# Seven block products for w2 in both halves of a fused attention and MLP kernel, two steps at a time

## The chip, the core and the metric

The kernel runs on one core of a Trainium2 chip. The time is that of the device in microseconds (us). Five engines work side by side, each with its own queue in program order: PE (matmuls; its weight loads are the row PEld), DVE and ACT (elementwise work, both read PSUM), POOL (elementwise work on SBUF) and SP, which here issues nearly all DMAs. Semaphores alone hold an engine back.

## The reference

With S = 2048 rows, D = 576 columns and F = 4608 hidden columns, float32:

```
x = A_x
g = sigmoid((x * gate_w).sum(-1))
a = linear_attention(x, wqkv, wo)        # 32 heads of 18 columns
y = layernorm(x)
h = gelu(y @ w1 + b1)
b = h @ w2 + b2
out = g * a + (1 - g) * b
```

## The kernel before

**Precision.** An operand is split in a high part (rounded to the matmul's format, by ACT) and a low part (the rest, subtracted by DVE). A product is the sum of high x high, high x low and low x high (`TERMS`).

**Stages.** A sweep over the 16 row tiles makes keys, queries and sums; `at(n, ...)` places jobs in it, among them four pairs of row tiles of normalised x (`load_pair`, `normal_pair`, `sum_pair`, `split_pair`, `store_pair`). Each pair is split and stored to `yd` in DRAM. Then comes attention, one row tile per turn of a loop; `extra[i]` places jobs after turn i. Then the MLP: 36 steps k. The first 18 go over w1's 18 chunks of 256 hidden columns for rows 0 to 1023 (first half), the other 18 over the same chunks for rows 1024 to 2047 (second half).

**The product with w1** is done in blocks of two by two with seven products in place of eight (Strassen's scheme): for each, `product` issues seven matmuls of 512 columns with an operand of `wa` or `wb` (w1) and one of `Y`. Four PSUM banks go round: X takes products 1, 6, 7 and 4, with copies by ACT between; Yb takes 2, Z takes 5 and 3. The operands of w1 are loaded (`load_w1`), summed on POOL (`sum_w1`), split (`split_w1`) and stored to `w1d` in the first half, and read back in the second.

**The product with w2** runs one step behind. In the first half `down` adds it for each of eight row tiles: 12 matmuls of 288 columns into a pair of banks, which DVE adds to `acc[s]`, attention's result, scaled by 1 - g. The steps 18 to 33 of the second half use seven products here too: POOL sums blocks of w2 (`sum_w2`) and of h (`sum_h`), ACT and DVE split them, `unit` issues six matmuls, and DVE (in the first step ACT for some) adds each result to `sums` in SBUF. The steps 34 and 35 are done plainly at the end, and `add_combined` puts the sums together. Attention's rows of the second half wait in DRAM (`late_acc`).

**Order.** Every engine gets its instructions in the order of the code. In the first half the other four pairs of row tiles are made between the down products (`after`).

Of the kernel before, what the change touches and what calls it, by code (L numbers as in the profile page):

```python
# [17 lines left out]
P = 128  # L18
# [16 lines left out]
GATES = ((0, 8), (8, 16))  # L35
EPS_PHI = 1e-6
# [76 lines left out]
def tile_gated_mix(ctx: ExitStack, tc: tile.TileContext, x, xm, xe, wm, we, wvm, wve, wo, um, ue, w2, b1, b2, gw, out):  # L113
# [39 lines left out]
    for _ in range(WARM):  # L153
# [11 lines left out]
    sums = {n: accs[:, i * TPB * HALF:(i + 1) * TPB * HALF].rearrange("p (s n) -> p s n", n=HALF)  # L165
            for i, n in enumerate(DOWN_ORDER)}
# [11 lines left out]
    late_acc = dram.tile([TPS, P, D], F32, name="late_acc")  # L178
# [205 lines left out]
    rows = spare[:, :4 * P].rearrange("p (a n) -> p a n", a=2)  # L384
    yr = spare[:, 4 * P:25 * P].rearrange("p (m s n) -> p m s n", m=7, s=3)

    def load_pair(sup, j):
        q = sup * TPS + 2 * j
        for a, m in enumerate((B11, B12)):
            i = ORDER[q + a]  # L390
            own = yr[:, m:m + 2]
# [161 lines left out]
    for j, (scaled, loaded, *parts) in enumerate(((9, 13, 18, 19, 20, 21), (14, 20, 25, 27, 28, 29),  # L553
                                                  (22, 28, 33, 34, 35, 36), (27, 35, 41, 42, 44, 45))):
        prepare_scale(j, scaled)
        at(loaded, load_pair, 0, j)
        for a in range(2):
            for k in range(2):
                at(loaded + 3 + a, normal_pair, 0, j, a, k)
        for m in range(4):  # L560
            at(parts[m // 2], sum_pair, 0, j, m)
        for part, n in enumerate(parts):
            at(n, split_pair, 0, j, part, lambda part=part: y_stages[part])
            at(n, split_tails, 0, j, part)
# [174 lines left out]
    def attend_out(i):  # L739
        act.activation(halves(acc[i]), abank[i][:, :, :HALF], AF.Identity, scale=g[:, PLACE[i]:PLACE[i] + 1])  # L740
        if i >= TPS:
            sp.dma_start(late_acc[i - TPS], acc[i])


    hs, c2s, w2raw = {}, {}, {}

    def wr(k):
        at_ = fresh[:, :24 * P] if k > 1 else spare[:, :24 * P]
# [38 lines left out]
    def w2_rows(k):  # L787
        c = k % NCHUNK
        return w2[c * CF * P:(c + 1) * CF * P].rearrange("(f p) d -> p f d", p=P)

    def load_w2(k, to):
        w2raw[k] = to.rearrange("p (f n) -> p f n", f=CF)
        sp.dma_start(w2raw[k], w2_rows(k))

    def split_w2(k, to, parts=(0, 1)):
        c2 = c2s[k] = to.rearrange("p (a f n) -> p a f n", a=2, f=CF)
        if 0 in parts:
            act.activation(c2[:, 0], w2raw[k], AF.Copy)
# [15 lines left out]
    def kept(p):  # L814

        t = up.tile([P, SB], F32, name="u")
        act.activation(t, p, AF.Copy)
        return t

    def plus(t, p):  # L820
        dve.tensor_tensor(out=t, in0=p, in1=t, op=OP.add)
        return t

    def gelu(k, f, t, src, whole, h=None, split=True):

        bias = b1s[:, k % NCHUNK * CF + f:k % NCHUNK * CF + f + 1]
        if split:
            h = hs[k, f, t] = take_h((k, f, t)) if h is None else h
            act.activation(h[:, 0], src, AF.Gelu_apprx_tanh, bias=bias)
        act.activation(whole, src, AF.Gelu_apprx_tanh, bias=bias)  # L830
        return lambda: dve.tensor_sub(h[:, 1], whole, raw(h[:, 0]))

    TERMS = ((0, 0), (0, 1), (1, 0))
    terms = [(f, a, w) for f in range(CF) for a, w in TERMS]

    def add(i, to, term):
        dve.scalar_tensor_tensor(to, term, omg[:, PLACE[i]:PLACE[i] + 1], to, op0=OP.mult, op1=OP.add)

    def down_terms(p, s, k, half, only=range(len(terms)), opens=True, closes=True):
        c0 = s % TPB * P  # L840
        for n in only:
            f, a, w = terms[n]
            pe.matmul(p, hs[k, f, s // TPB][:, a, c0:c0 + P], c2s[k][:, w, f, half_cols(half)],
                      start=opens and n == 0, stop=closes and n == len(terms) - 1)

    def down(k, s):

        if k >= 0:
            p = two_of(ff_pairs)[:, :, :HALF]
            for n in range(len(terms)):  # L850
                for half in range(2):
                    down_terms(p[:, half], s, k, half, (n,))
            if s % TPB == TPB - 1:
                give_back_h((k, 0, s // TPB), (k, 1, s // TPB))
            add(s, halves(acc[s]), p)
            if k == 1 + s:
                add(s, acc[s], b2b)
            if k == HALF_TIME - 1:
                sp.dma_start(out[s * P:(s + 1) * P, :], acc[s])
        for job in later.get((k + 1, s), ()):  # L860
            job()

# [44 lines left out]

    fresh = ctx.enter_context(tc.tile_pool(name="fresh", bufs=1)).tile([P, 33 * P], F32, name="fresh")
    region = ctx.enter_context(tc.tile_pool(name="region", bufs=1)).tile([P, 56 * P], F32R, name="region")
    y_stage = [region[:, n * 10 * P:(n + 1) * 10 * P].rearrange("p (m s n) -> p m s n", m=2, s=5) for n in range(2)]  # L910
    w2_whole = fresh[:, 24 * P:33 * P]
    c2_places = [region[:, (20 + 18 * n) * P:(38 + 18 * n) * P] for n in range(2)]
    w2_sums = fresh[:, :7 * HALF].rearrange("p (m n) -> p m n", n=HALF)
    s_places = [region[:, 14 * HALF + n * 2 * SB:][:, :2 * SB].rearrange("p (a n) -> p a n", a=2)
                for n in range(3)]
    load_w2(0, w2_whole)

    later = {}

    def after(k, s, f, *args):  # L920
        later.setdefault((k + s // 8, s % 8), []).append(lambda: f(*args))

    for j in range(TPB):
        k, s = divmod(15 + 28 * j, TPS)
        after(k, s, load_pair, 1, j)
        for n in range(4):
            after(k, s + 6 + n, normal_pair, 1, j, n // 2, n % 2)
            after(k, s + 10 + n, sum_pair, 1, j, n)
        for part in range(4):
            after(k, s + 14 + 3 * part, split_pair, 1, j, part, lambda part=part: y_stage[part % 2])  # L930
            after(k, s + 15 + 3 * part, split_tails, 1, j, part)
# [13 lines left out]
    for k in range(HALF_TIME):  # L945
        X, Yb, Z = bank(), bank(), bank()
        if k:
            split_w1(k, False)
# [275 lines left out]
```

## Time and profile before

| | us |
|---|---|
| median of 3 runs (1125.62 to 1129.38) | 1129.38 |
| the profiled execution | 1128.42 |
| its span, first to last instruction | 1126.7 |

Line numbers in the profile mean little here, since a helper on one line records every operation (L109): groups go by tiles. A group's row gives the operation, out<-in with shapes, its count, busy us, mean ns of one, and idle time ahead of it with what ended it. A row of the timeline gives the start, the time to the last one's end, engine, operation and count. A row by stages gives the stage, its length, then busy us and count for PE, PEld, DVE, ACT and POOL, the granted clock, the DMA engines' share and GB/s. `spare`, `acc` of the first half and `sums` are parts of the tile `accs`; raw w1 and w2 lie in `fresh`.

### The profile page before, as it was taken

Reading aid. Unit: us, or ns where it says so; the run is one execution under the profiler, and the core shown is the slowest. Engines: PE = TensorE matmul, PEld = TensorE weight load, DVE = VectorE, ACT = ScalarE, POOL = GpSimd, SP = SyncE. Lnnn points to the kernel's source line nnn. Section 1 sums busy time; section 2 is a strip of 40 time slices with the busy share of each in tenths; the row PEclk is TensorE's granted clock in tenths of the full one; section 3 lists DMA queues with packets and bytes.
Section 4 is the critical chain, followed back from the end, with each engine's and each line's share of the span. In section 5 each row is a group of like instructions: output and inputs, shape, how many; then the busy total and the mean of one; then the engine's idle time right before and its main releaser. Section 6 shows DMA issues by size and latency. Waiting matters only on the chain.

```text
span 1126.7 us, 18078 instructions
## 1 busy us (share of the span) xinstructions
PE 1114.1 (99%) x6867; PEld 1022.0 (91%) x6867; DVE 861.9 (76%) x1297; ACT 545.5 (48%) x933; POOL 308.6 (27%) x255
## 2 busy tenths in 40 slices
PE   8999999999999999999999999999999999999998
PEld 8999988999899999999999999988999899989988
DVE  4567776885678878778768765678898889888985
ACT  6566655443545444535544543455444544454441
POOL 1111112342111123112122111234453445344520
PEclk9999999999999999999999999999999999999999
DMA  6466765834455764555655549744444444444452
GB/s 175 148 115 176 175 164 99 298 120 143 168 168 179 234 209 160 205 172 190 235 193 174 190 166 390 286 134 124 122 136 137 120 123 137 134 121 124 137 175 84
DMA packets 106252, 189.84 MB, mean 168 GB/s; under 512 B 12351, under 2 KB 61247, under 8 KB 101942
## 3 DMA queue, kind: packets, MB, share of 16 engines
q1 hardware_dynamic: 105602, 188.10, 53.3%
q8 instruction: 54, 0.88, 0.3%
q10 hardware_dynamic: 564, 0.59, 0.2%
q14 instruction: 32, 0.26, 0.1%
HBM read 121.93 MB, written 66.73 MB: 167 GB/s over the span
## 4 chain that ended last, share of the span: by engine, by line
PE 90%; DMA 3%; DVE 3%; ACT 2%; issue 1%; SPq 1%; ACTq 0%
PE ps L109 90%; DMA t<-in_xe 2%; DMA accs<-in_xe 1%; DVE accs L109 1%; SPq L109 1%; DVE u L109 0%; DMA s<-in_wm 0%; DVE region L109 0%; ACT y L109 0%; ACT h L109 0%; ACT u L109 0%; DVE ys L109 0%; DVE wp L109 0%; ACT e L109 0%; DVE den L109 0%
## 5 line engine op out<-in xcount | busy, mean ns | idle before, releaser
L109 PEld LDWEIGHTS ps<-region,h 128*128 128x128 f32 x2568 | 368.5, 188 | 22.7 <-DVE accs L109 1.0
L109 PE MATMUL ps<-region,h 128*128 128x288 f32 x2568 | 383.1, 295 | 0.5 <-DVE region L109 0.2
L109 PE MATMUL ps<-y,wa 128*128 128x512 f32 x1008 | 265.0, 392 | 0.0
L109 POOL TENSOR_TENSOR fresh<-fresh 128x384 f32<-128x384 f32 (+1 forms) x128 | 136.9, 1075 | 439.0 <-DMA fresh<-in_ue 277.0
L109 PE MATMUL ps<-y,wb 128*128 128x512 f32 x756 | 200.9, 394 | 1.0 <-ACT u L109 1.0
L109 PEld LDWEIGHTS ps<-y,wa 128*128 128x128 f32 x1008 | 177.8, 188 | 26.2
L109 DVE TENSOR_TENSOR accs<-ps,accs 128x576 f32<-128x576 f32 x210 | 158.2, 753 | 32.3 <-PE ps L109 22.6
L109 ACT ACTIVATE h<-u,b1s 128x512 fp32r<-128x512 f32 x90 | 65.3, 725 | 214.7 <-DVE u L109 214.7
L109 PEld LDWEIGHTS ps<-y,wb 128*128 128x128 f32 x756 | 132.9, 188 | 23.0 <-ACT u L109 1.7
L109 DVE SCALAR_TENSOR_TENSOR accs<-ps,omg,accs 128x576 f32<-128x576 f32 (+1 forms) x146 | 118.2, 810 | 44.3 <-PE ps L109 43.3
L109 ACT ACTIVATE u<-ps 128x512 f32<-128x512 f32 x108 | 63.8, 591 | 150.2 <-PE ps L109 150.0
L109 POOL TENSOR_TENSOR u<-u 128x512 f32<-128x512 f32 x64 | 100.3, 1567 | 126.1 <-ACT u L109 122.3
L109 PE MATMUL ps<-y 128*128 128x288 f32 (+1 forms) x896 | 127.5, 300 | 2.8 <-ACT y L109 1.6
L109 PEld LDWEIGHTS ps<-y 128*128 128x128 f32 x896 | 124.4, 192 | 5.3 <-ACT y L109 2.3
L109 DVE TENSOR_TENSOR h<-u,h 128x512 fp32r<-128x512 f32 x142 | 104.7, 737 | 27.3 <-ACT u L109 27.1
L109 ACT ACTIVATE u<-u,b1s 128x512 f32<-128x512 f32 x108 | 78.2, 724 | 53.9 <-DVE u L109 50.9
L109 DVE TENSOR_TENSOR u<-ps,u 128x512 f32<-128x512 f32 x108 | 74.2, 687 | 36.5 <-ACT u L109 23.4
L109 PEld LDWEIGHTS ps<-region 128*128 128x128 f32 x600 | 90.3, 188 | 8.9 <-ACT accs L109 0.5
L109 DVE TENSOR_TENSOR region<-fresh,region 128x576 fp32r<-128x576 f32 (+1 forms) x83 | 82.0, 987 | 20.7 <-ACT region L109 19.2
L109 PE MATMUL ps<-region 128*128 128x288 f32 x600 | 96.2, 295 | 0.1
L109 PE MATMUL ps<-wp,qt 128*128 128x288 f32 x448 | 63.3, 298 | 0.3 <-DVE qt L109 0.3
L109 PEld LDWEIGHTS ps<-wp,qt 128*128 128x128 f32 x448 | 59.9, 188 | 0.5 <-DVE qt L109 0.5
(131 smaller groups left out, 1039.6 us busy)
## 6 DMA issues: line engine op xcount, KB each, us to landing
w1d<-wa SPq DMA_DIRECT2D x18, 1280.0 KB
wa<-w1d SPq DMA_DIRECT2D x72, 320.0 KB
y<-yd SPq DMA_DIRECT2D x14, 1280.0 KB
w1d<-wb SPq DMA_DIRECT2D x18, 960.0 KB
wb<-w1d SPq DMA_DIRECT2D x54, 320.0 KB
fresh<-in_w SPq DMA_DIRECT2D x20, 576.0 KB
fresh<-in_w SPq DMA_DIRECT2D x32, 288.0 KB
fresh<-in_um SPq DMA_DIRECT2D x64, 128.0 KB
```

Source lines behind the costliest of these rows:

```text
L109: return lambda *args, **kwargs: self.tc.keep_in_program_order(op(*args, **kwargs))
```

## The change

- `unit` now serves both halves. Two steps make a window of 14 slots, one product with w1 each; a window's units are those of the window before. A unit adds both steps (j = 0, 1) in PSUM, 12 matmuls of 288 columns, before DVE adds it to its place in `accs`. The last window alone is done plainly.
- h is kept whole for two steps in `ups`. Gelu runs once, not twice; ACT's high part and DVE's low part are made for both steps in one instruction, 1024 wide, in two operand places used in turn; those of w2 likewise (576 wide). POOL sums h in the first half too.
- In each slot the six matmuls of j = 0 stand inside the product with w1, but after product 7 both pieces stand behind it.
- Attention's rows of both halves go to `late_acc` and come back at the end of each half, in `w1_raw`.
- All eight pairs of row tiles are made ahead: five in the sweep, two in attention (POOL normalises them), the last in the first window, which has no units. The load of w1 for step 1 moves from attention to that window.

The core of the diff:

```diff
+PAIRS_IN_SWEEP = 5
...
-        sp.dma_start(late_acc[i - TPS], acc[i])
+        sp.dma_start(late_acc[i], acc[i])
...
+    def unit(p, x, j):
+        m, q = divmod(x, 2)
+        if j == 0:
+            unit_bank[p, x] = two_of(ff_pairs)[:, :, :HALF]
+        to, place = unit_bank[p, x], (7 * p + m) % 2
+        for i, (a, b) in enumerate(TERMS):
+            for n in range(2):
+                c0 = (2 * q + n) * P
+                pe.matmul(to[:, n], h_ops[:, place, j, a, c0:c0 + P], w2_ops[:, place, b, j],
+                          start=j == 0 and i == 0, stop=j == 1 and i == len(TERMS) - 1)
...
+    for k in range(HALF_TIME):
+        w, odd = divmod(k, 2)
+        if k:
+            do(w, (1, 7)[odd], split_w1, k, False)
+            do(w, (3, 9)[odd], store_w1, k, False)
+        if k + 1 < HALF_TIME:
+            do(w, (1 if k else 0, 7)[odd], load_w1, k + 1)
+            do(w, (3, 9)[odd], sum_w1, k + 1)
+            do(w, (5, 11)[odd], split_w1, k + 1, True)
+            do(w, (6, 13)[odd], store_w1, k + 1, True)
...
+        for m in range(7):
+            do_first(w, 2 * m - 2, prepare_hi, p, m)
+            do(w, 2 * m - 2, prepare_h_lo, p, m)
+            do(w, 2 * m - 2, prepare_w2_lo, p, m)
+        for x, m in ((0, S3), (3, S2), (6, S1), (7, S4)):
+            do(w, x, sum_h, p, m)
...
+    for w in range(WINDOWS):
+        for x in range(14):
+            k, i = 2 * w + x // 7, x % 7
...
+            product(k, n, into[n], n in (1, 2, 5), range(0, 4))
+            run_jobs(w, x, 0)
+            if w and n != 7:
+                unit(w - 1, x, 0)
+            product(k, n, into[n], n in (1, 2, 5), range(4, 7))
+            finish_up(k, n, into)
+            if w:
+                for j in range(n != 7, 2):
+                    unit(w - 1, x, j)
+                unit_out(w - 1, x)
+            run_jobs(w, x, 1)
```

Three places show how instructions move. On SP, around the loads of raw w1 for the second step (`in_um`, `in_ue`), before:

```order
L109 DMA w1d_112<-wa 128x2560
L109 DMA late_acc<-acc_87 128x576
L109 DMA late_acc<-acc_88 128x576
L109 DMA accs<-in_um 128x2x128
L109 DMA accs<-in_ue 128x1x128
```

and in the changed kernel:

```order
L111 DMA late_acc<-acc_94 128x576
L111 DMA w_raw<-in_um 128x2x128
L111 DMA w_raw<-in_ue 128x1x128
...
L111 DMA accs<-moments_111 128x512
L111 DMA w1d_112<-wa 128x2560
L111 DMA w2r<-in_w 128x2x288 x4
L111 DMA w1d_112<-wb 128x1920
```

The loads stood after the store of attention's tenth row tile (`acc_88`). Now they stand after that of the last (`acc_94`) and ahead of the row factors (`moments`), the stores of w1 for the first step and w2. The first of them waits for the stores of the last rows, which lie in the memory that `w_raw` takes.

On POOL, from the end of attention (`qz` are products for a row tile's weights) into the MLP, before:

```order
L109 TENSOR_TENSOR qz<-acc_93,pks 128x576
L109 TENSOR_TENSOR qz<-acc_94,pks 128x576
L109 TENSOR_TENSOR accs<-accs 128x384 x4
L109 TENSOR_TENSOR fresh<-fresh 128x384 x64
L109 TENSOR_TENSOR fresh<-fresh 128x288 x4
```

and in the changed kernel:

```order
L111 TENSOR_TENSOR accs<-accs 128x768
L111 TENSOR_TENSOR qz<-acc_94,pks 128x576
L111 TENSOR_TENSOR accs<-accs 128x384 x8
L111 TENSOR_TENSOR accs<-accs 128x768
L111 TENSOR_TENSOR w_raw<-w_raw 128x384 x4
L111 TENSOR_TENSOR accs<-accs 128x768 x3
L111 TENSOR_TENSOR accs<-accs 128x384 x4
L111 TENSOR_TENSOR w_raw<-w_raw 128x384 x4
L111 TENSOR_TENSOR w2r<-w2r 128x576 x4
L111 TENSOR_TENSOR u<-u 128x512 x2
```

Where sums of w1 alone filled the first half, normalising the last pair (768 wide), its sums (384) and those of w2 (576) and h (512) now stand in one queue with them; one 768 stands ahead of the sums for step 1.

On DVE, a piece of the first half, before (one step in part):

```order
L109 TENSOR_TENSOR h<-u,h 128x512
L109 TENSOR_TENSOR wa<-fresh,wa 128x4x256
L109 TENSOR_TENSOR wa<-fresh,wa 64x4x128
L109 TENSOR_TENSOR u<-ps,u 128x512
L109 SCALAR_TENSOR_TENSOR accs<-ps,omg,accs 128x576
L109 TENSOR_TENSOR accs<-accs 128x768
```

and in the changed kernel:

```order
L111 TENSOR_TENSOR h<-u,h 128x2x512
L111 TENSOR_TENSOR w_ops<-w2r,w_ops 128x576
L111 TENSOR_TENSOR accs<-ps,accs 128x576
L111 TENSOR_TENSOR wa<-w_raw,wa 128x4x256
L111 TENSOR_TENSOR wa<-w_raw,wa 64x4x128
L111 TENSOR_TENSOR u<-ps,u 128x512
L111 TENSOR_TENSOR accs<-ps,accs 128x576
L111 TENSOR_TENSOR h<-u,h 128x2x512
L111 TENSOR_TENSOR w_ops<-w2r,w_ops 128x576
```

The low parts of h are twice as wide, those of w2 stand behind each, and evictions of units (`accs<-ps,accs`) take the place of `down`'s additions.

More of the change, by code (lines that the diff above doesn't have):

```diff
@@ L812, in product @@
                 load_split_w1(k + 1, a)
[L814 to L861, printed above, removed]
+    upper = accs[:, spare.shape[1]:]
     weigh(3)
@@ L909, in tile_gated_mix @@
[L909 to L931, printed above, removed]
-            after(k, s + 16 + 3 * part, store_pair, 1, j, part)
@@ new lines, in add, with load_late, add_combined @@
+    def add(i, to, term):
+        dve.scalar_tensor_tensor(to, term, omg[:, PLACE[i]:PLACE[i] + 1], to, op0=OP.mult, op1=OP.add)
+    late_tiles = [w1_raw[:, n * D:(n + 1) * D] for n in range(5)] + [pks, b2b]
+    def load_late(i, place):
+        sp.dma_start(late_tiles[place], late_acc[i])
+    def add_combined(p, i, place):
+        s = i % TPS
+        m0, m1 = (SLOTS[p // HALF_PAIRS][n] for n in ((2, 3), (4, 7))[s // TPB])
+        c = accs.rearrange("p (m s n) -> p m s n", m=7, n=HALF)[:, :, s % TPB]
+        add(i, halves(late_tiles[place]), c[:, m0:m1 + 1:m1 - m0])
@@ L958, in tile_gated_mix @@
-        low11 = gelu(k, 0, 0, u1, u1)
-        down(k - 1, 1)
-        low11()
-        product(k, 6, X, False)
-        u2 = kept(X)
-        if k:
-            split_w2(k, c2_places[k % 2])
-        if k < HALF_TIME - 1 and k:
-            load_w2(k + 1, w2_whole)
-            sum_w1(k + 1)
-        elif k:
-            load_w2_blocks(k + 1)
-            for n in range(4):
-                sum_w2(n)
-        down(k - 1, 2)
-        product(k, 5, Z)
-        if not k:
-            split_w1(1, True)
-            store_w1(1, True)
@@ L1061, in add_combined @@
-    def add_combined(s):
-        c = accs.rearrange("p (m s n) -> p m s n", m=7, n=HALF)[:, :, s % TPB]
-        m0, m1 = (DOWN_ORDER.index(n) for n in ((2, 3), (4, 5))[s // TPB])
-        add(TPS + s, halves(late_tiles[s]), c[:, m0:m1 + 1:m1 - m0])
-    def add_sums(engine, to, x):
-        engine.tensor_tensor(out=sums[to], in0=sums[to], in1=sums[x], op=OP.add)
-    late_tiles = [fresh[:, n * D:(n + 1) * D] for n in (0, 1, 4, 5, 6)] + [pks, b2b, accs[:, 0:D]]
-    UP_ORDER = (1, 2, 6, 5, 7, 4, 3)
@@ new lines, in tile_gated_mix, with down_terms @@
+    run_jobs(WINDOWS, 0, 0)
+    run_jobs(WINDOWS, 0, 1)
+    p = WINDOWS - 1
+    tail_pairs = cycle((next(ff_pairs), next(ff_pairs), 0, 2))
+    def down_terms(to, s, half):
+        terms = [(f, j, a, b) for f in range(CF) for j in range(2) for a, b in TERMS]
+        c0 = s % TPB * P
+        for n, (f, j, a, b) in enumerate(terms):
+            w = w2_tail(((B11, B12), (B21, B22))[f][half])
+            yield lambda n=n, f=f, j=j, a=a, b=b, w=w: pe.matmul(
+                to, h_tail((f, s // TPB))[:, j, a, c0:c0 + P], w[:, b, j], start=n == 0, stop=n == len(terms) - 1)
@@ L1164, in tile_gated_mix @@
     for s in range(TPS):
         i, to = TPS + s, late_tiles[s]
-        if s >= len(held):
-            add_combined(s)
-        steps = (LAST,) if s < len(held) else (PLAIN, LAST)
+        pair = two_of(tail_pairs)[:, :, :HALF]
+        add_combined(p, i, s)
         if s < TPS - 1:
-            p = held[s] if s < len(held) else two_of(ff_pairs)[:, :, :HALF]
-            for k in steps:
-                for n in range(len(terms)):
-                    for half in range(2):
-                        down_terms(p[:, half], s, k, half, (n,), k == PLAIN, k == LAST)
-            add(i, halves(to), p)
-            if s == 0:
-                lows[3]()
-            sp.dma_start(out[i * P:(i + 1) * P, :], to)
+            for both in zip(*(down_terms(pair[:, half], s, half) for half in range(2))):
+                for mm in both:
+                    mm()
+            add(i, halves(to), pair)
+            store_out(i, s)
@@ L1179, in tile_gated_mix @@
         else:
             for half in range(2):
-                p = bank()[:, :HALF]
-                for k in steps:
-                    down_terms(p, s, k, half, opens=k == PLAIN, closes=k == LAST)
-                add(i, to[:, half_cols(half)], p)
+                for mm in down_terms(pair[:, half], s, half):
+                    mm()
+                add(i, to[:, half_cols(half)], pair[:, half])
                 sp.dma_start(out[i * P:(i + 1) * P, half_cols(half)], to[:, half_cols(half)])
```

459 lines of the change are left out of this document (228 added, 231 removed).

## The prediction

> **What bounds the kernel now.** The page's busy row and its chain that ended last come first, then the waits of PE.
>
> ```profile
> PE 1114.1 (99%) x6867; PEld 1022.0 (91%) x6867; DVE 861.9 (76%) x1297; ACT 545.5 (48%) x933; POOL 308.6 (27%) x255
> PE 90%; DMA 3%; DVE 3%; ACT 2%; issue 1%; SPq 1%; ACTq 0%
> ```
>
> PE is busy for 99% of the span and holds 90% of the chain. A busy PE alone proves little, since its ends are modelled, so the waits decide:
>
> ```profile
> PE ps L109 <- DMA accs<-in_gw: 2.2, 1, 2.2
> PE ps L109 <- ACT y L109: 1.6, 2, 1.5
> ```
>
> The longest wait of PE in the whole run is 2.2 us, at the start. Five stages matter here: most of the sweep over the row tiles, attention, first half, the last step of that half, and second half. In each row: length, then busy us of PE, PEld, DVE, ACT and POOL, clock, DMA share and GB/s.
>
> ```profile
> 62.00:165.00 103.00, 101.93 (x681) 97.53 (x680) 74.87 (x160) 63.53 (x147) 17.00 (x14) 1.00 0.67 164
> 206.20:278.20 72.00, 71.68 (x552) 71.45 (x553) 57.36 (x96) 31.98 (x71) 24.87 (x20) 1.00 0.54 208
> 338.80:674.10 335.30, 335.30 (x2032) 306.24 (x2031) 262.75 (x352) 161.02 (x213) 70.29 (x56) 1.00 0.57 191
> 674.10:698.10 24.00, 24.00 (x148) 21.93 (x147) 14.57 (x20) 10.33 (x15) 0.84 (x2) 1.00 1.00 384
> 813.20:1061.50 248.30, 248.30 (x1465) 223.87 (x1465) 219.55 (x310) 117.39 (x198) 108.74 (x88) 1.00 0.44 129
> ```
>
> PE is full in each of them. DVE is next: 262.75 of 335.3 us in the first half (78%), 219.55 of 248.3 in the second (88%). So matmuls taken away are worth their whole pace, as long as no other engine makes PE wait instead.
>
> **Term 1, the matmuls.** Before, first-half products with w2 take 18 steps of 8 x 2 x 6 = 96 matmuls, second-half units 16 steps of 84, and the two last steps 96 each: 3264. Afterwards 17 windows of two steps take 7 x 2 x 2 x 6 = 168 and the last window 192: 3048. So 216 of 288 columns go. Their pace, from PE's timeline:
>
> ```profile
> 701.28 1.77 PE L109 MATMUL ps<-y,wa 128*128 128x512 f32 x7
> 702.89 1.75 PE L109 MATMUL ps<-region,h 128*128 128x288 f32 x12
> 704.48 1.77 PE L109 MATMUL ps<-y,wa 128*128 128x512 f32 x7
> ...
> 851.80 1.19 PE L109 MATMUL ps<-y,wb 128*128 128x512 f32 x4
> 852.83 0.96 PE L109 MATMUL ps<-region 128*128 128x288 f32 x6
> ...
> 858.30 1.09 PE L109 MATMUL ps<-y,wa 128*128 128x512 f32 x4
> 859.23 0.95 PE L109 MATMUL ps<-region,h 128*128 128x288 f32 x6
> ```
>
> From start to start, twelve take 704.48 - 702.89 = 1.59 us, 0.1325 each; seven of 512 columns take 1.61. 216 x 0.1325 = **-28.6 us**.
>
> **Term 2, a small wait.** At 851.80 four matmuls last 1.03 us to the next start, elsewhere (858.30) 0.93: product 4 waits 0.1 us for ACT's copy of the bank that product 7 filled, with only one piece of six matmuls between. Afterwards both pieces (1.59 us) stand behind product 7. 16 such steps: **-1.6 us**.
>
> **Term 3, the first window.** It has no units, so its two steps are 98 products of 512 columns with nothing between. Here PE has least cover, and more is moved in. The rows of the same place before:
>
> ```profile
> 271.23 8.31 SPq L109 DMA_DIRECT2D late_acc<-acc  x3
> 278.17 6.55 PE L109 MATMUL ps<-y,wa 128*128 128x512 f32 x28
> 278.45 0.74 ACT L109 ACTIVATE acc<-ps,g 128x576 f32<-128x576 f32 x1 [2.96 <-PE ps L109]
> 284.36 1.49 ACT L109 ACTIVATE wa<-accs 128x1536 fp32r<-128x1536 f32 x1
> 285.88 1.94 DVE L109 TENSOR_TENSOR wa<-accs,wa 128x1024 fp32r<-128x1024 f32 x2 [1.29 <-ACT wa L109]
> 290.34 1.76 PE L109 MATMUL ps<-y,wa 128*128 128x512 f32 x7
> 292.97 0.46 SPq L109 DMA_DIRECT2D fresh<-in_um  x1
> 296.88 0.53 SPq L109 DMA_DIRECT2D fresh<-in_ue  x1
> 301.93 5.18 POOL L109 TENSOR_TENSOR fresh<-fresh 128x384 f32<-128x384 f32 x4 [34.74 <-DMA fresh<-in_ue]
> ```
>
> A step without down products takes 290.34 - 278.17 = 12.2 us. Of it 1.0 us is waiting for copies (seven products at 1.61 make 11.2), which the second step now has too: +1.0. The w1 blocks of step 1 were loaded and summed during attention; now their load stands behind the last store of attention rows, in memory that such rows leave. The last row is ready at 279.2, SP has issued its store at 279.5; the landing isn't in the trace, and I put it 2 us later (between 0 and 4.5, what the load below takes at its end). Eight issues of w1 take 292.97 to 297.41, and POOL's first sum starts at 301.93: 9.0 us from first issue to first sum. 281.5 + 9.0 = 290.5. POOL has one sum of normalised x ahead (768 wide, row factors loaded behind w1; about 1 us of it remains), then two sums that wa needs (5.18 for four, so 2.6; I take 2.3): 293.8. ACT's split 1.49, DVE's two subtractions 1.94: 297.2. Two matmuls can run first (0.4): 296.8, where PE is ready at 290.3 + 1.0. **5.5 us**. The next step's sums queue on POOL behind three more 768-wide sums (1.85 each, an estimate between 1.46 for 576 and 2.80 for 1152 elements, below), four of 384 and the rest of the former: about 308.6, and 3.4 more to the operands, less 0.4: 311.6, PE ready at 296.8 + 12.2 = 309.0: 2.6. The first unit's operands are split behind that: 1.2. Step 0 itself is split at row tile 14 of 16, not 7: 1.2. While it waits, SP holds the row factors, the stores of w1 and w2's load behind it; POOL's wait holds ACT's split, and behind that ACT's copies of X, for which PE waits. Sum **+11.5**; 5 if the store lands at once and POOL keeps ahead, 15 if each comes late.
>
> The Trainium skill, page "TensorE: Matmul & The Clock Gate", Part 1, says that PE idle for about 3.4 us falls to half its clock until it has been busy as long. No run here shows it (2.2 us is the longest wait, PEclk is full). By it the 5.5 us wait would cost up to 1.7 more, an estimate, and the sum would be 1120.
>
> **Term 4, windows 1 to 8.** Splitting both operands, sums of h and of w2 now lie in the first half too, beside the splitting of w1. Costs from groups of instructions (mean ns after the bar):
>
> ```profile
> L109 DVE TENSOR_TENSOR accs<-ps,accs 128x576 f32<-128x576 f32 x195 | 146.9, 754 | 30.9 <-PE ps L109 21.7 <-ACT region L109 1.9
> L109 DVE TENSOR_TENSOR wa<-fresh,wa 128x1024 fp32r<-128x1024 f32 x16 | 19.5, 1220 | 0.0
> L109 DVE TENSOR_TENSOR wa<-fresh,wa 64x512 fp32r<-64x512 f32 x16 | 11.0, 689 | 0.5
> L109 DVE TENSOR_TENSOR wb<-fresh,wb 128x768 fp32r<-128x768 f32 x16 | 15.2, 951 | 0.0
> L109 DVE TENSOR_TENSOR wb<-fresh,wb 64x384 fp32r<-64x384 f32 x16 | 8.9, 555 | 0.5
> L109 POOL TENSOR_TENSOR u<-u x64: 1289/1657/1697, 722.8 to 1067.9; 128x512 f32<-128x512 f32 x64
> L109 POOL TENSOR_TENSOR fresh<-fresh x63: 805/1022/2128, 330.2 to 699.3; 128x384 f32<-128x384 f32 x60, 128x288 f32<-128x288 f32 x3
> L109 POOL TENSOR_TENSOR pks<-pks,k 128x576 f32<-128x576 f32 x15 | 21.8, 1456 | 102.6 <-DVE k L109 102.5
> L109 POOL TENSOR_TENSOR accs<-accs 128x1152 f32<-128x1152 f32 x3 | 8.4, 2802 | 20.6 <-DVE accs L109 20.6
> ```
>
> Window of PE: 14 x (1.61 + 1.59) = 44.8 us. DVE in it: 14 evictions of 0.75, 6 additions of 0.69, 7 low parts of h (1024 wide, 1.22) and of w2 (576, 0.75), two splits of w1 (3.4 each): 35.2 us, 79%. POOL: 8 sums of h at 1.29, 8 of w1 at 1.02, 4 of w2 at 1.46: 24.3. ACT has 14 copies and gelus of 0.6 to 0.73, 14 high parts and two splits, under 27. So none is over 44.8 alone; without waits the term is 0. But DVE and POOL hinder each other:
>
> ```profile
> 1072.35 3.06 POOL L109 TENSOR_TENSOR accs<-accs 128x1152 f32<-128x1152 f32 x1 [2.81 <-DVE accs L109]
> 1073.68 2.28 DVE L109 TENSOR_TENSOR region<-u,region 128x512 fp32r<-128x512 f32 x1
> 1076.55 0.68 DVE L109 TENSOR_TENSOR h<-u,h 128x512 fp32r<-128x512 f32 x1
> ```
>
> A DVE subtraction with both inputs in SBUF takes 0.68 alone, and 2.28 when it starts 1.3 us into a POOL sum: it ends 0.55 after that sum's end. In the second half before, such DVE work and POOL's sums fill about 16 of 22.6 us per step, and PE doesn't wait. Here they make 20.6 + 24.3 = 44.9 of 44.8. Units wait for the low parts, which wait for POOL. I bound the cost at 0 and 4 us per window (a wait of one POOL sum, 1.3, for about three of the operands); the nearest row is the second half, 88% DVE and no wait, so I take 0.75: 8 x 0.75 = **+6**.
>
> **Term 5, the rest.** A fifth pair of row tiles goes through the sweep: by the widths above four DVE instructions of 0.95, four of 0.56, four splits of up to 0.69 and four of about 0.5, some 10 us where DVE has 28 of 103 free, which hides them. Two pairs go through attention: 4 to 5 us more on DVE, which has 14.6 of 72 free, and on POOL 8 x 1.85 + 8 x 1.02 = 23 us, free 47. In both stages the queues are in order, so some waits may show: 0 to 5, I take 1.5. At half time seven reloads of Y share DMAs that are busy to 1.00 for a step in which PE waits for nothing; the step is 1.6 us shorter and w2's load in it twice as large, against which the output's stores leave: 0 to 3, I take 0.5. Half as many evictions per step free DVE, which has no price on PE's path; the tail keeps its 192 matmuls. **+2** (0 to 8).
>
> **Sum.** -28.6 - 1.6 + 11.5 + 6 + 2 = -10.7. The profiled execution took 1128.4 (span 1126.7 and 1.7 around it), 1.0 below the median of 1129.4: **1118**, -0.9%. About 0.5%, 5.6 us, can be told from no change, so the lines are 1122.8 and 1134.0.
>
> **Rivals.**
> *The cover holds*: the first window costs its 5, the others nothing: 1128.4 - 30.2 + 5 = 1103. For it, DVE at 88% without one wait. Against it, POOL's queue in the first window: 4 x 1.85 + 12 x 1.02 + 4 x 1.46 = 25.5 us of sums in 24.4.
> *The shared inputs of DVE and POOL bound windows 1 to 8*: 44.9 of 44.8 us of operations that exclude each other leave no room for their order. At 4 us per window, half in window 8 (one split of w1 less), that is 30 in place of 6: 1142, slower than before. It decides from 3.0 us per window on. For it, the 2.28 us row. Against it, POOL can run while DVE empties PSUM (14.6 us per window). The Trainium skill, page "SBUF — State Buffer", "SBUF: two separate sides", calls that port pair an exclusive lock held for the whole instruction; the row above agrees, and by it this rival follows.
> *Earlier stages lose*: sweep and attention give back 8, the first window 15: 1126, no change.
>
> **How the numbers follow.** Forecast (1110 to 1128) 0.46; cover holds 0.15; the port 0.24; earlier stages 0.15. Faster: 0.15 + 0.36 + 0.03 = 0.54. Same: 0.10 + 0.10 + 0.03 = 0.23. Slower: 0.21 of the port, 0.02 of the last: 0.23. The range takes the first rival's time and all but the port's worst: 1102 to 1143.
>
> **What would show it.** 216 fewer matmuls at the same pace; steps of 22.4 us from window 9 on; a PE wait of 4 to 7 us some 12 us after attention, ended by DVE's wa, and one of 2 to 3 a step later; windows 1 to 8 of 45 to 46.5 us (49 by the port) with waits for h or w_ops. Wrong it is if windows 9 to 16 are longer than 45, or the sweep ends over 5 us later.

## The result, and the profile after

The changed kernel takes 1204.88 us (median of 4 runs, 1202.17 to 1211.01) where the kernel before takes 1129.22: a ratio of 1.0686, 95% interval 1.0636 to 1.0735. It is slower by 6.9%, outside the range of the prediction. The profiled execution took 1206.92 us, its span is 1205.2.

The page's busy row and its chain that ended last, of the kernel after:

```profile
PE 1125.5 (93%) x6651; PEld 1019.0 (85%) x6651; DVE 874.2 (73%) x1108; ACT 569.0 (47%) x911; POOL 536.3 (45%) x359
PE 55%; DVE 19%; DMA 10%; POOL 6%; issue 4%; ACT 3%; SPq 3%; POOLq 0%; ACTq 0%; DVEq 0%
```

The 216 matmuls are gone (6867 to 6651), but PE holds 55% of the chain in place of 90%, and DVE, DMA and POOL have what it lost. Where, the rows by stage show: window 0, window 1, windows 2 to 8, windows 9 and 10, windows 11 to 16, the next step, and the last step with the tail (length, then busy us of PE, PEld, DVE, ACT and POOL, clock, DMA share, GB/s).

```profile
282.43:319.74 37.31, 26.70 (x100) 19.38 (x99) 18.32 (x26) 17.63 (x24) 20.89 (x16) 0.91 0.82 301
319.74:376.66 56.92, 49.17 (x267) 43.24 (x267) 43.56 (x39) 31.04 (x43) 34.34 (x23) 0.91 0.45 152
376.66:757.64 380.98, 342.61 (x1864) 302.08 (x1863) 291.99 (x294) 172.13 (x224) 212.68 (x140) 0.94 0.43 148
757.64:851.60 93.96, 90.49 (x534) 81.24 (x533) 72.93 (x75) 43.81 (x63) 45.55 (x26) 1.00 0.68 233
851.60:1122.78 271.18, 269.96 (x1599) 244.02 (x1598) 179.46 (x204) 122.21 (x169) 111.47 (x72) 1.00 0.44 129
1122.78:1145.23 22.45, 22.45 (x136) 20.35 (x134) 14.18 (x17) 10.86 (x15) 11.92 (x7) 1.00 0.45 129
1145.23:1205.18 59.95, 51.51 (x327) 48.13 (x325) 44.37 (x45) 14.50 (x20) 13.83 (x6) 0.94 0.26 95
```

Beside what the prediction's terms give for each stage (window 0: 12.2 + 11.2 and 1.0, 5.5 and 1.2 of term 3; window 1 its other 3.8; a window 44.84, twice an undisturbed step of 22.42 us, and 0.75 of term 4 up to the eighth; the last row 22.4, the 42.65 of before from 1084.05 on and 84 matmuls more at 0.1325):

| stage | forecast us | measured us | more |
|---|---|---|---|
| up to the MLP | 279.7 | 282.4 | 2.8 |
| window 0 | 31.1 | 37.3 | 6.2 |
| window 1 | 49.4 | 56.9 | 7.5 |
| windows 2 to 8 | 319 | 381.0 | 62.0 |
| windows 9, 10 | 90.2 | 94.0 | 3.8 |
| windows 11 to 16 | 269 | 271.2 | 2.2 |
| the rest | 76.2 | 82.4 | 6.2 |

Two thirds of the miss lie in windows 2 to 8, which last 54.4 us each in place of 45.6. PE's waits there, by what ended them:

```profile
PE ps L111 <- DVE w_ops L111: 20.3, 9, 2.9
PE ps L111 <- DVE wa L111: 16.9, 8, 2.4
```

One step of each window begins with a wait for `wa`, the other with one for the first unit's operands (`w_ops`), 2.2 to 2.9 us each. One of the first kind, followed back through the timelines of the engines in window 4:

```profile
498.08 1.54 DVE L111 TENSOR_TENSOR wb<-w_raw,wb 128x768 fp32r<-128x768 f32 x2 [1.05 <-ACT wb L111]
...
499.07 0.37 SPq L111 DMA_DIRECT2D w_raw<-in_um  x1
499.65 0.55 SPq L111 DMA_DIRECT2D w_raw<-in_ue  x1
...
503.39 5.25 POOL L111 TENSOR_TENSOR w_raw<-w_raw 128x384 f32<-128x384 f32 x4 [11.52 <-DMA w_raw<-in_ue]
508.60 6.50 POOL L111 TENSOR_TENSOR u<-u 128x512 f32<-128x512 f32 x4
...
510.44 0.69 ACT L111 ACTIVATE u<-ps,b1s 128x512 f32<-128x512 f32 x1 [4.08 <-POOL u L111]
511.03 1.48 ACT L111 ACTIVATE wa<-w_raw 128x1536 fp32r<-128x1536 f32 x1
...
512.59 3.06 DVE L111 TENSOR_TENSOR wa<-w_raw,wa 128x1024 fp32r<-128x1024 f32 x2 [2.67 <-POOL u L111]
...
515.71 0.74 PE L111 MATMUL ps<-y,wa 128*128 128x512 f32 x2 [2.42 <-DVE wa L111]
```

Read it backwards. PE waits for DVE's split into `wa`; that waits for ACT's. ACT has stood 4.08 us in front of a gelu whose place in `u` a sum of h on POOL must leave first. POOL had that sum behind w1's sums, which waited 11.52 us for raw w1. The last two loads of raw w1 go out at 499.07, when the split into `wb` has read the block that they overwrite, and that split stands two slots into the step. So raw w1, with one buffer, closes a loop of load, sums and split through four queues. It did before too, but POOL had little else to do, and the sums began earlier. POOL in the step of before that starts at 506.47:

```profile
517.10 6.01 POOL L109 TENSOR_TENSOR fresh<-fresh 128x384 f32<-128x384 f32 x4 [14.57 <-DMA fresh<-in_ue]
```

That is 10.6 us into the step; 503.39 above is 18.9 us into one that starts at 484.50.

The other kind, the wait of 2.87 us for `w_ops` that ends at 489.20, stands behind DVE's low parts for the first unit:

```profile
482.06 6.48 POOL L111 TENSOR_TENSOR w2r<-w2r 128x576 f32<-128x576 f32 x3
485.61 1.67 DVE L111 TENSOR_TENSOR h<-u,h 128x1024 fp32r<-128x1024 f32 x1
487.20 1.95 DVE L111 TENSOR_TENSOR w_ops<-w2r,w_ops 128x576 fp32r<-128x576 f32 x1
```

Beside POOL's sums they take 1.67 and 1.95 us, where 1.22 and 0.75 were put, and they begin late, behind a split of `wa` that ends at 484.9.

A third thing goes with these waits. PE's timeline behind another one:

```profile
460.87 0.73 PE L111 MATMUL ps<-y,wa 128*128 128x512 f32 x2 [2.40 <-DVE wa L111]
461.44 0.95 PE L111 MATMUL ps<-w_ops,h 128*128 128x288 f32 x6
462.23 1.42 PE L111 MATMUL ps<-y,wa 128*128 128x512 f32 x3
463.45 1.64 PE L111 MATMUL ps<-w_ops,h 128*128 128x288 f32 x6
464.89 1.49 PE L111 MATMUL ps<-y,wa 128*128 128x512 f32 x4
466.22 0.96 PE L111 MATMUL ps<-w_ops,h 128*128 128x288 f32 x6
```

From start to start, six of 288 columns take 0.79 us at 461.44 and at 466.22, but 1.44 at 463.45; three of 512 take 1.22 at 462.23, where 0.69 is usual. The granted clock there (stretch, length, busy us of the engines, then clock, DMA share, GB/s):

```profile
460.87:462.20 1.33, 1.33 (x8) 1.24 (x9) 1.33 (x3) 0.63 (x1) 1.33 (x2) 1.00 0.53 216
462.40:465.40 3.00, 3.00 (x11) 2.62 (x11) 2.83 (x3) 1.71 (x3) 0.81 (x1) 0.50 1.11 328
```

PE runs at half its clock for some 3.4 us and loses 1.6 (0.53 + 0.65 in these two pieces, 0.41 in the next). Fourteen such stretches in windows 2 to 8 make 22 us; the granted clock of 0.94 over 381 us says 23. They start at 380.37, 407.67, 434.98, 462.29 and so on, 27.31 us apart each time, which is eight times 3.41. So they keep to a beat of 3.41 us and not to the end of a wait: at 380.89 the clock is halved already when PE resumes, at 460.87 only 1.4 us later.

And the turns of DVE and POOL show in the groups of the kernel after (busy us, mean ns):

```profile
L111 POOL TENSOR_TENSOR u<-u 128x512 f32<-128x512 f32 x136 | 217.4, 1625 | 129.6 <-DVE h L111 83.7
L111 DVE TENSOR_TENSOR h<-u,h 128x1024 fp32r<-128x1024 f32 x119 | 173.3, 1456 | 5.1 <-ACT h L111 5.0
L111 DVE TENSOR_TENSOR w_ops<-w2r,w_ops 128x576 fp32r<-128x576 f32 x119 | 138.8, 1166 | 0.0
```

The prediction had them at 1.29, 1.22 and 0.75 us. Together windows 2 to 8 have DVE busy for 292 us and POOL for 213 of 381; what the order makes of it, the runs must tell.

### The profile page after: what moved, and what is told of

It reads as the page before. It is cut to its first block, busy times and chain, and to the rows that moved or that the text cites. A ratio compares the mean times of both kernels' runs of the same rounds, so it can differ in the third digit from the quotient of the medians.

```text
span 1205.2 us, 17894 instructions
## 1 busy us (share of the span) xinstructions
PE 1125.5 (93%) x6651; PEld 1019.0 (85%) x6651; DVE 874.2 (73%) x1108; ACT 569.0 (47%) x911; POOL 536.3 (45%) x359
## 4 chain that ended last, share of the span: by engine, by line
PE 55%; DVE 19%; DMA 10%; POOL 6%; issue 4%; ACT 3%; SPq 3%; POOLq 0%; ACTq 0%; DVEq 0%
PE ps L111 55%; DVE wa L111 5%; DVE h L111 3%; DMA yd<-ys 3%; POOL w_raw L111 3%; SPq L111 3%; DVE w_ops L111 3%; POOL u L111 3%; DMA w_raw<-in_ue 2%; DMA w_raw<-in_um 2%; DVE accs L111 2%; DVE u L111 1%; DVE wb L111 1%; ACT wa L111 1%; DMA accs<-moments 1%
## 5 line engine op out<-in xcount | busy, mean ns | idle before, releaser
L111 PEld LDWEIGHTS ps<-w_ops,h 128*128 128x128 f32 x2856 | 441.5, 194 | 78.9 <-DVE w_ops L111 34.3
L111 PE MATMUL ps<-w_ops,h 128*128 128x288 f32 x2856 | 470.6, 302 | 32.3 <-DVE w_ops L111 29.7
L111 POOL TENSOR_TENSOR u<-u 128x512 f32<-128x512 f32 x136 | 217.4, 1625 | 129.6 <-DVE h L111 83.7
L111 PEld LDWEIGHTS ps<-y,wa 128*128 128x128 f32 x1008 | 183.3, 199 | 56.9 <-DVE wa L111 32.5
L111 DVE TENSOR_TENSOR h<-u,h 128x1024 fp32r<-128x1024 f32 x119 | 173.3, 1456 | 5.1 <-ACT h L111 5.0
L111 POOL TENSOR_TENSOR w2r<-w2r 128x576 f32<-128x576 f32 x68 | 123.3, 1813 | 103.0 <-DMA w2r<-in_w 59.2
L111 POOL TENSOR_TENSOR w_raw<-w_raw 128x384 f32<-128x384 f32 x68 | 77.8, 1155 | 175.9 <-DMA w_raw<-in_ue 134.0
L111 ACT ACTIVATE h<-u 128x1024 fp32r<-128x1024 f32 x119 | 125.1, 1051 | 45.4 <-PE ps L111 45.2
L111 DVE TENSOR_TENSOR w_ops<-w2r,w_ops 128x576 fp32r<-128x576 f32 x119 | 138.8, 1166 | 0.0
L111 ACT ACTIVATE w_ops<-w2r 128x576 fp32r<-128x576 f32 x119 | 79.7, 669 | 0.0
L111 DVE TENSOR_TENSOR wa<-w_raw,wa 128x1024 fp32r<-128x1024 f32 (+1 forms) x34 | 58.5, 1719 | 28.3 <-ACT wa L111 18.7
```

Source lines behind the costliest of these rows:

```text
L111: return lambda *args, **kwargs: self.tc.keep_in_program_order(op(*args, **kwargs))
```

## The experiments

Three theories, as the expectations name them. A: the loop through raw w1's one buffer, its load late. B: DVE and POOL exclude each other at their inputs in SBUF, and have too much of that work in a window. C: the units' sums are held on POOL behind w1's waiting sums. All kernels start from the one after. Up to the first window they are mostly alike, yet reach it between 280.5 and 286.3 us, so stages are compared rather than times; the lengths are those of the rows by stage. In e7, e8, e9 and e12 windows 2 to 8 have the instructions of the kernel after and take 53.6 to 54.1 us against its 54.4, so less than 1 us there tells nothing.

| kernel | time | window 0 | window 1 | a window of 2 to 8 | a window of 11 to 16 |
|---|---|---|---|---|---|
| after (profiled) | 1206.9 | 37.3 | 56.9 | 54.4 | 45.2 |
| e1 wb early | 1195.0 | 37.8 | 60.2 | 52.2 | 45.3 |
| e2 no reload | 1158.0 | 37.4 | 55.5 | 47.8 | 45.2 |
| e3 no h sums | 1165.7 | 36.9 | 53.6 | 49.4 | 45.1 |
| e4 unit sums first | 1182.3 | 37.8 | 53.7 | 51.3 | 45.2 |
| e5 = e2 and e3 | 1146.1 | 36.6 | 53.0 | 46.3 | 45.1 |
| e6 reordered | 1165.5 | 39.8 | 52.9 | 48.6 | 45.4 |
| e7 late adds on DVE | 1209.5 | 37.8 | 58.8 | 54.1 | 45.4 |
| e8 w1 work in second half | 1224.6 | 36.8 | 58.7 | 53.6 | 48.7 |
| e9 one engine each | 1204.7 | 37.9 | 57.0 | 53.6 | 46.0, 45.0 |
| e10 further order | 1164.9 | 40.6 | 53.2 | 48.4 | 45.3 |
| e11 = e6 without h sums | 1142.7 | 40.8 | 49.1 | 45.8 | 45.4 |
| e12 no last pair | 1204.6 | 36.7 | 58.6 | 54.1 | 45.1 |

Each is one run. The kernel before, run beside them, took 1127.6 to 1132.6.

**e1, the split into `wb` and the load behind it earlier.**

```diff
-            do(w, (1, 7)[odd], split_w1, k, False)
+            do(w, (-1, 6)[odd], split_w1, k, False)
...
-            do(w, (1 if k else 0, 7)[odd], load_w1, k + 1)
+            do(w, (-1 if k else 0, 6)[odd], load_w1, k + 1)
```

> Only the order changes: the split of raw w1 into wb, and the load behind it, stand at the end of the step before (two product slots earlier in even steps, one in odd ones). Theory A, a loop through the one buffer of raw w1 (wb's split frees the buffer, the load, POOL's sums and wa's split follow, and the next step's products wait for wa): the loop gets 6.4 and 3.2 us shorter, the waits of 2.8 to 3.1 us for wa and w_ops go, windows 1 to 8 take 45 to 48 us each in place of 54.7, and the time is 1125 to 1155. Theory B, that DVE and POOL have too much to do with inputs in SBUF that they can only read by turns: the operations are the same, windows stay above 53, the time above 1195.

Measured 1195.0, 52.2 us a window: closer to what B says, though 2.2 us of each window go. In window 5 w1's sums start 11.2 and 13.4 us into the steps, where the kernel after has 18 to 19 in window 4, but ACT's split into `wa` still stands behind a gelu that waits (2.53 us, until 557.79). PE's waits for `wa` fall to 1.2 us at most, those for `w_ops` grow from 20.3 to 24.1 us in all. The load alone is not the loop's only limit.

**e2, no reload of raw w1.**

```diff
+            if k < 2:
                 do(w, (1 if k else 0, 7)[odd], load_w1, k + 1)
```

> Leaves out the loads of raw w1 from step 3 on (the blocks of step 2 are summed and split again in each step). Theory A: nothing to wait for ahead of POOL's sums, windows 1 to 8 at 45 to 48 us, time 1125 to 1155. Theory B: DVE and POOL have all their operations, windows above 52, time above 1185.

**e3, no sums of h in the first half.**

```diff
+            if p >= HALF_PAIRS - 1:
                 do(w, x, sum_h, p, m)
```

> Leaves out POOL's sums of h in the first half (8 of 1.3 us per window, a third of POOL's work there). Theory A: the loop of raw w1 stays, windows 1 to 8 at 50 to 54 us, time 1165 to 1200. Theory B: POOL has 14 us per window left where DVE has 20 with inputs in SBUF, so they fit: 45 to 47 us, 1125 to 1150.

**e4, POOL's order.**

```diff
-            do(w, (3, 9)[odd], sum_w1, k + 1)
...
+    for k in range(HALF_TIME - 1):
+        do(k // 2, (3, 10)[k % 2], sum_w1, k + 1)
```

> Only POOL's order changes: the sums of h and w2 due in the same slots stand ahead of w1's sums (one of h in even steps, two of w2 in odd ones). Theory C, that it is the units' sums held on POOL behind w1's waiting sums that cost the time: the waits for w_ops and most of those for wa go, windows 1 to 8 at 46 to 49 us, time 1135 to 1160. Theory A: the load still ends as late; only ACT's wait for one sum of h goes, 0 to 2.5 us per window, time 1183 to 1207. Theory B: no change, 1200 to 1210.

The rows of windows 2 to 8 in e2, e3 and e4:

```profile
374.18:708.46 334.28, 320.58 (x1865) 284.93 (x1864) 284.67 (x294) 172.13 (x224) 202.10 (x136) 1.00 0.36 136
```
```profile
370.98:717.09 346.11, 326.29 (x1865) 293.00 (x1863) 261.90 (x294) 172.11 (x224) 117.64 (x84) 0.97 0.47 161
```
```profile
373.79:733.10 359.31, 329.75 (x1864) 293.52 (x1863) 280.77 (x294) 172.27 (x224) 206.49 (x138) 0.97 0.46 156
```

Per window they save 6.7, 5.0 and 3.1 us of the 9.6 over 44.8. e2 nearly does what A says (its time 3 us above); e3 lies between A and B; e4 between A and C. No theory holds alone: the saved parts of e2 and e3 already exceed the whole. With the load away (e2) the clock is back at 1.00, yet 2.9 us a window stay, with all of DVE's and POOL's work.

**e5, both left out** (the edits of e2 and e3 together).

> Leaves out both: the loads of raw w1 from step 3 on, and POOL's sums of h in the first half. If the late load (theory A) and the turns of DVE and POOL at their inputs (theory B) are the two causes, nothing is left to wait for: windows 1 to 8 at 44.8 to 46.5 us, time 1122 to 1140. If another wait stands behind them, windows stay at 47 to 49 us, time above 1140.

46.3 us a window, inside the first answer near its edge, with the time 6 above it, since window 1 still takes 53.0 us and window 0 36.6. So load and turns make all but 1.5 of the 9.6 us.

**e6, order alone.** wb's split and the load at the end of the step before, behind the unit's low parts due there; the store of `wa` behind that load; some units' sums ahead of w1's.

```diff
-            do(w, (1, 7)[odd], split_w1, k, False)
...
-            do(w, (1 if k else 0, 7)[odd], load_w1, k + 1)
-            do(w, (3, 9)[odd], sum_w1, k + 1)
...
+                do(w, (-1, 6)[odd], split_w1, k, False)
...
+                do(w, (-1 if k else 0, 6)[odd], load_w1, k + 1)
...
+            do(w, (3, 10)[odd], sum_w1, k + 1)
             do(w, (5, 11)[odd], split_w1, k + 1, True)
-            do(w, (6, 13)[odd], store_w1, k + 1, True)
+            do(w, (8, 15)[odd], store_w1, k + 1, True)
```

> Order only, nothing left out: wb's split and the load of raw w1 at the end of the step before, the store of wa behind that load, and the units' sums of one or two slots ahead of w1's on POOL. If the late load and the held queue make most of the waits (A with C): windows 1 to 8 at 45.5 to 49 us, time 1130 to 1163. If DVE and POOL exclude each other too often whatever the order (B): windows at 50 to 53 us, time 1168 to 1195.

Windows 2 to 8 and PE's waits there:

```profile
373.18:713.41 340.23, 324.48 (x1865) 284.35 (x1864) 274.88 (x294) 171.35 (x224) 198.03 (x136) 1.00 0.46 162
```
```profile
PE ps L111 <- DVE wa L111: 10.5, 7, 1.5
PE ps L111 <- DVE w_ops L111: 3.8, 8, 0.6
```

48.6 us, as A with C says, on its upper side; the time, 1165.5, is 2.5 above. With all work in place, the order alone takes 5.8 us from each window, somewhat less than leaving out the load (6.7). e1 and e4, its two main parts, had taken 2.2 and 3.1. No wait is longer than 1.5 us, and the clock is 1.00. 3.8 us stay.

**e8, the amount alone.** Windows 11 to 16, which hardly wait, get w1's POOL sums and DVE subtractions of the first half, on memory that nothing else uses.

```diff
+    for w in range(11, 17):
+        for x in (3, 9):
+            do(w, x, more_sums, 2048)
+        for x, n in ((1, 768), (5, 1024), (7, 768), (11, 1024)):
+            do(w, x, more_splits, n)
```

> Adds to windows 11 to 16 as many POOL sums and DVE subtractions of the same widths as w1 has in the first half, on memory that nothing else uses there: no load, no ACT, and no PE waits for them. These six windows take 271.2 us together without them. Theory B: DVE and POOL now have the amounts of the first half, so waits for w_ops come by that alone, 2 to 4 us per window, 283 to 296 us together, time 1217 to 1230. Theory A alone: no loop, so no waits, 271 to 275 us, time 1203 to 1209.

The six windows (without the work: 851.60:1122.78 above), PE's waits in them, and one of these in the timeline:

```profile
846.81:1138.90 292.09, 273.77 (x1599) 245.59 (x1597) 245.82 (x251) 120.46 (x169) 186.68 (x120) 0.99 0.41 119
```
```profile
PE ps L111 <- DVE w_ops L111: 18.3, 12, 1.8
```
```profile
867.24 7.45 POOL L111 TENSOR_TENSOR u<-u 128x512 f32<-128x512 f32 x4
...
871.36 2.20 DVE L111 TENSOR_TENSOR h<-u,h 128x1024 fp32r<-128x1024 f32 x1
...
873.48 1.82 DVE L111 TENSOR_TENSOR w_ops<-w2r,w_ops 128x576 fp32r<-128x576 f32 x1
...
875.36 0.80 PE L111 MATMUL ps<-w_ops,h 128*128 128x288 f32 x4 [1.59 <-DVE w_ops L111]
```

20.9 us more in six windows, 3.5 each, with no load, no loop and no PE waiting for the added work. While POOL makes four sums, DVE's two low parts take 2.20 and 1.82 us in place of 1.22 and 0.75, and POOL's sums 1.86 in place of 1.29: each waits for one of the other's to end. So semaphores are not all that holds an engine back here. B has its price, and it is close to what e6 has left (3.8) and e2 (2.9).

**e9, which engine.** The same work taken apart: POOL's in windows 11 to 13, DVE's in 14 to 16.

```diff
-    for w in range(11, 17):
+    for w in range(11, 14):
         for x in (3, 9):
             do(w, x, more_sums, 2048)
+    for w in range(14, 17):
         for x, n in ((1, 768), (5, 1024), (7, 768), (11, 1024)):
```

> The added work of the second half taken apart: windows 11 to 13 get only POOL's eight sums of 384, windows 14 to 16 only DVE's subtractions. With both, each window took 48.0 to 50.4 us; with neither, 45.2. If it is the sum of both engines' work on inputs in SBUF that decides (theory B: it is then 38 and 37 us of 44.8, not 45), either alone costs under 1 us a window: 45 to 46 us in all six. If DVE's own amount of work makes the waits, windows 14 to 16 stay at 47.5 to 50 and 11 to 13 fall to 45. If sums of h held behind others on POOL make them, windows 11 to 13 stay at 47.5 to 50 and 14 to 16 fall to 45.

Windows 11 to 13, then 14 to 16:

```profile
845.63:983.62 137.99, 136.07 (x801) 122.13 (x799) 97.84 (x101) 60.97 (x85) 87.16 (x60) 1.00 0.44 126
983.62:1118.71 135.09, 134.75 (x801) 121.98 (x799) 112.92 (x127) 60.55 (x84) 59.39 (x36) 1.00 0.45 129
```

46.0 and 45.0 us a window, where both together take 48.7 and neither 45.2. Neither DVE's work alone nor POOL's queue alone makes the waits; both together do. The Trainium skill, page "SBUF — State Buffer", "SBUF: two separate sides", calls the shared port pair an exclusive lock; the rows of e8 agree (2.20 us in place of 1.22).

**e7, the late additions.** Seven additions of 1152 elements put the sums together at half time, and seven in the tail; two and five of them were POOL's.

```diff
-        for x, by, n, t in ((4, pool, 2, 1), (10, eng, 6, 1), (10, eng, 7, 6), (11, pool, 4, 7), (12, dve, 6, 5),
-                            (12, eng, 7, 5), (14, dve, 3, 6)):
+        for x, by, n, t in ((4, dve, 2, 1), (10, dve, 6, 1), (10, dve, 7, 6), (11, dve, 4, 7), (12, dve, 6, 5),
+                            (12, dve, 7, 5), (14, dve, 3, 6)):
```

> The additions of 1152 elements by which the sums are put together at half time and in the tail (four and eight... of them on POOL) all go to DVE, 1.36 us each there. Theory B in its narrow form, that each such POOL operation of 3 us holds DVE's next one until it ends: the waits of PE of 4.1 us in the tail and 2.1 us at half time go, time 1193 to 1200. If DVE just has too much work at those places, more work makes them longer: 1206 to 1212.

The tail of the kernel after, whose longest wait this was to shorten:

```profile
1155.89 9.85 POOL L111 TENSOR_TENSOR accs<-accs 128x1152 f32<-128x1152 f32 x3 [9.17 <-DVE accs L111]
...
1160.23 3.03 DVE L111 TENSOR_TENSOR h<-u,h 128x1024 fp32r<-128x1024 f32 x1
...
1163.19 3.16 DVE L111 TENSOR_TENSOR w_ops<-w2r,w_ops 128x576 fp32r<-128x576 f32 x1
...
1166.40 1.33 PE L111 MATMUL ps<-w_ops,h 128*128 128x288 f32 x4 [3.82 <-DVE w_ops L111]
```

The last step and tail fall from 59.95 to 57.51 us; the wait of 3.8 us is gone, and one of 2.0 for DVE's `u` takes its place. Windows 9 and 10 don't move (93.96 to 94.06; PE waits 3.5 us in them without the edit and 3.3 with it). The time, 1209.5, lies where the second answer has it, but tells little, since this run reached the first window 3.8 us later than the profiled one. So the turns explain 2.4 of the 6.2 us over forecast in the tail. The clock of 0.94 over its 59.95 us, 3.6 us, is about as much as the rest; half time's share is not settled.

**e10, the order further,** on top of e6 (its other edits: the late additions on DVE, raw w1 in memory that other rows leave).

```diff
-            do(w, (3, 10)[odd], sum_w1, k + 1)
-            do(w, (5, 11)[odd], split_w1, k + 1, True)
+            do(w, (2, 10)[odd], sum_w1, k + 1)
+            do(w, (4, 11)[odd], split_w1, k + 1, True)
...
-    do(0, 0, split_w1, 0, False)
+    do(0, 2, split_w1, 0, False)
...
-        do(0, 2 + n, normal_pair, 1, 3, n % 2, n // 2, pool)
+        do(0, 4 + n // 2, normal_pair, 1, 3, n % 2, n // 2, pool)
```

> Order only, nothing left out, on top of the reordered loads and sums: in even steps w1's sums one slot earlier, ahead of the sums of h, and wa's split one slot earlier; in the first window wb's split of step 0 two slots later, w1's sums ahead of the normalising of the last pair, raw w1 in memory that other rows leave; the late additions on DVE. Theory A with C (what is left of waits for wa, 1.9 us in odd steps, is the queue ahead of wa's split): windows 2 to 8 fall from 48.6 to 46 to 47.5 us, the first window from 39.8 to 31 to 37, the tail by 2 to 3, time 1135 to 1152. Theory B alone: DVE and POOL do the same work, windows stay at 48 to 49, time 1152 to 1165.

48.4 us a window and 1164.9: what B says. What e6 left is not the queue's order. Window 0 did not get shorter, 40.6.

**e11, e6 without the sums of h.**

> On top of the reordered loads and sums (48.6 us a window): leaves out POOL's sums of h in the first half, so that DVE's and POOL's work on inputs in SBUF is 35 us a window in place of 45. If the late load with its queue (gone by the order) and the sum of both engines' work (now below what made waits) are the two causes, and nothing stands behind them: windows 2 to 8 at 44.8 to 45.8 us, time 1137 to 1145. With another wait behind: 46.5 and more.

```profile
370.63:691.13 320.50, 317.54 (x1864) 284.67 (x1863) 258.22 (x294) 171.21 (x224) 111.98 (x81) 1.00 0.49 172
```

45.8 us, the upper end of the first answer. With the loop mended and 10 us of POOL's work away, 1.0 us of the 9.6 is left.

**e12, the last pair of row tiles not made in window 0.**

```diff
-    for n in range(4):
-        do(0, 2 + n, normal_pair, 1, 3, n % 2, n // 2, pool)
-        do(0, 6 + n // 2, sum_pair, 1, 3, n, pool)
...
-        do(0, x, part_of, 1, 3, part, stage)
+        do(0, x, store_other, part, stage)
```

> The kernel after, without the making of the last pair of row tiles in the first window (its normalising and sums on POOL and its splits on ACT and DVE; stale blocks are stored in their place). Windows 0 and 1 took 37.3 and 56.9 us. If that work stands in the way of w1's sums and splits there: window 0 at 29 to 33, window 1 at 52 to 55, time 1190 to 1198. If it is the late load of w1 for step 1 (behind the stores of attention's last rows) alone: window 0 at 35.5 to 37.5, window 1 at 55 to 57, time 1202 to 1207.

36.7 and 58.6 us: window 0 as the second answer says, window 1 longer than either. The work is not what holds the first window: its waits for step 1 get shorter (1.3 and 1.3 us in place of 2.3 and 3.1), but those for step 2's `wa` grow to 4.2 and 2.2 (0.6 and 2.7). POOL now stands idle for 17.3 us until raw w1 for step 2 has come (314.90), so with that work gone the load holds the window. No run here shows what would shorten it.

## Why the prediction was wrong, point by point

**Terms 1 and 2 held.** 216 matmuls went, and an undisturbed step of the second half takes 22.42 us (851.60 to 874.02) in place of 22.57 (0.15 for the small wait, 0.1 forecast). With PE's small waits for `w_ops` the mean of windows 11 to 16 is 22.60.

**Term 3 held in its mechanism.** Window 0's waits of PE:

```profile
PE ps L111 <- DVE wa L111: 3.9, 2, 3.1
PE ps L111 <- ACT u L111: 3.9, 4, 1.6
PE ps L111 <- ACT wa L111: 2.3, 1, 2.3
```

The wait for step 1's `wa`, put at 5.5 us, is 2.3 + 3.1, and the load goes out 2.3 us after the last store's issue, as worked out. Waits for ACT's copies came to 3.9 in two steps, not 1.0 in each: the place of the first copy in `u` held a row of attention, and ACT waited 2.30 us until its store had landed, which the prediction had reckoned with for the load alone. A clock of 0.91 over 37.3 us costs 3.4 more. These two make 5.3 of the 6.2 us over forecast. The prediction named the Trainium skill's page "TensorE: Matmul & The Clock Gate", Part 1, and kept its half rate out of the sum, as a wait that no run had shown. The runs show it, and already for 1.8 to 2.9 us of idle PE, where the page has about 3.4.

**Term 4 is the step that failed:** 6 us for windows 1 to 8, where some 75 came. It held that "none is over 44.8 alone; without waits the term is 0", and priced only the turns. Two things were wrong with it.

First, no row of it followed raw w1 around its one buffer. That the split into `wb` and the load behind it had moved from one product into a step (ACT's part at 508.15, 1.7 us in) to two slots was in the code; the load's last two issues now go out 14.6 us into a step (499.07), before it was 5.9 (512.32). That POOL's sums for the units then queue behind sums that wait for that load, and ACT's gelus behind those, was not looked for in these windows, though term 3 did just that for window 0. e6 prices it: 5.8 us a window (5.0 against the shortest of the unchanged ones, 53.6), 41 in windows 2 to 8, of which some 23 are the half clock that its long waits bring. The 7.5 us of window 1 are not taken apart.

Second, the price of the turns, "the nearest row is the second half, 88% DVE and no wait, so I take 0.75". That row had 16 of 22.6 us filled; the new sum was 44.9 of 44.8. e8 and e9 show how the price rises in a window of 44.8: either engine's extra work alone, 37 to 38 us together with the rest, costs under 1 us, and both, 45 us, cost 3.5. The rival "shared inputs" had that rule and its price (4 us a window), and was given 0.24. Its price is near the measured 3.5 to 3.8; with the loop, which no rival had, the windows came out longer still, 9.6 us over 44.8.

**Term 5** was 2 and came to some 13 more: 2.8 by the start of the MLP, 3.8 at half time, 6.2 in the tail. The tail was taken as unchanged; its late additions on POOL hold DVE's low parts, which the kernel before didn't make there.

**Signs named.** The two waits for `wa` in the first window and behind it came, the first 15 us after attention, not 12. Steps of 22.4 us came in the second half where nothing waits. Windows 1 to 8 of 45 to 46.5 did not come, and 49 by the port is what they take once the order is mended. Windows 9 to 16 longer than 45 us, named as a sign of being wrong, came too: 47.0 each for 9 and 10, 45.2 for the others. The third rival's terms add up to some 1127, not 1126, which changes no chance.

**What the change is worth.** Two steps of before take 47.9 us. With the loop mended by order, a window takes 48.4 to 48.6: seven products instead of eight save 3.2 us of PE, and the turns of DVE and POOL take 3.5 to 3.8 back. Only with more work left out (e5, e11) is a window clearly shorter; e2's 47.8 is level. No version here was faster than the kernel before.

## What to carry to other kernels

Where two engines take turns at a resource, add their work and hold the sum against the period; each engine's own share says little. Here the cost rose from under 1 us to 3.5 between 38 and 45 us of work in 44.8. Follow each buffer that exists once around its loop (freed by what, loaded when, behind what in each queue) before calling the work on it covered. Price a wait of PE of 2 to 3 us with the half-rate stretch behind it.

## What was not expected of the hardware

The clock of PE was halved in whole beats of 3.41 us. From the trace of the kernel after (285 to 756 us), counted by that beat: where PE stood idle for 1.9 to 2.9 us of a beat at full clock, the next beat ran at 0.50; where it was 1.55 or less, the clock stayed at 1.00. So the wait of 2.39 us that ends at 354.53 cost no clock, since it fell on two beats with 0.92 and 1.47. In e8 (790 to 1140 us) an idle 1.84 us in one beat brought the half clock, the only time in windows 11 to 16, and 1.67 or less did not. This is read from these two traces; no experiment varied it.
